# All five engines of a fused HGRN2 and PReLU kernel in one new written order, DMA issues included

## The chip, the core and the metric

The kernel runs on one core of a Trainium2 chip. Its five engines work side by side, each through its own instructions in order: TensorE (PE, with its weight loads shown apart as PEld), VectorE (DVE), ScalarE (ACT), GpSimd (POOL) and SyncE (SP). SP issues only DMA transfers; POOL issues most loads of inputs and two transfers a step that add in flight; ACT issues a few transfers. The metric is device microseconds (us) from launch to end, lower is better.

## The reference

Inputs are `q`, `k`, `v`, `f_logit` of shape (4, 8, 768, 48), `w_in` (384 x 2048), `w_out` (2048 x 384) and `alpha` (2048). In fp32:

```python
f = 1.0 / (1.0 + np.exp(-f_logit))
for t in range(S):                                   # 768 positions
    state = f[:, :, t, :, None] * state + np.einsum('bhd,bhe->bhde', k[:, :, t], v[:, :, t])
    y[:, :, t] = np.einsum('bhd,bhde->bhe', q[:, :, t], state)
x = y.transpose(0, 2, 1, 3).reshape(3072, 384)
h = x @ w_in
g = np.maximum(h, 0.0) + alpha * np.minimum(h, 0.0)
return g @ w_out
```

## The kernel before

**Steps.** The 768 positions are cut into six chunks `c` of 128, the four batch entries into two pairs `bp` (U = 2). That makes twelve steps, numbered 0 to 11, chunk by chunk and within it pair 0 and pair 1; a step covers 256 tokens with all eight heads. The state of a pair lives in 48 partitions of the tile `vs0` or `vs1`, beside the 64 positions of `v` of a half chunk, so that one product gives both the part from earlier positions and the part from these.

**The attention of a step**, in the letters of the order: `e` loads f, q, k, v (POOL; SP in step 0). `f F g G h i k l q p` are decays, scans and scaled copies of q and k (ACT and DVE). `r0 r1` (line 582), `u0 u1` (L591, in the first two steps also L681) and `o` (L566) are PE products of q and k for pairs of positions at growing distance; their results go from PSUM through masked copies on DVE (`R`: L599; `U`: L451 or L702) or copies on ACT (`O`: L573; `H`: L688) into `ad` and `A` (`A`: L606). `K` turns the scaled keys by way of DRAM (four transfers `turned`, one `ksn`, all on SP); in steps 0 and 1 it is a copy on ACT of PE transposes (`k`: L713, `K`: L719). `d` (L539) multiplies them with `v`, `D` and `M` (L550, L554) move the state on. `y0`, `y1` (L614) are the final products for the pair's first and second batch entry, 32 matmuls each, both into one PSUM tile `py`; `Y0`, `Y1` (L494, in steps 0 and 1 L729) are the ACT copies of them into the tile `y`. `X` brings `y` into the layout `xT` in which PE needs it: by three PE products and three ACT copies in step 0 (L738, L747), by ten small transfers over SP, ACT and POOL in steps 1 and 11 (L626), else by two transfers to `tokens` in DRAM and one back (L503, L505, all SP).

**The dense part of a step**, letters after an `N`. `a0` to `a7` (L831) are eight products of `xT` with blocks of `w_in`, 12 matmuls of 256 columns in two instructions each, into a PSUM bank `ph`. `r` (L854) is the ACT part of the PReLU, `c` (L859) the two DVE instructions that finish it into `gate`. From step 3 on blocks 3 to 6 are done in three cheaper rounded passes: `x y z` (L817, L820) split `xT` on ACT, `Y Z` (L823) are POOL transfers that add to `xl` and `xs`, `a` does the first two passes, `q` (L844) scales the bank, `b` is the third pass. The second layer is 64 matmuls `p` (L866, banks `po`) in step 0. From step 1 on it is seven block products `p0` to `p6` (L886, banks `pa` to `pf`) with DVE sums `m u v w` ahead (L880) and `d e f h i j l L` behind (L896); `k g` (ACT), `s0 s1` (SP) finish and store. Weights come in eight pieces each: `a`, `b` hold the transfer (SP) and two ACT conversions (L281, L282), `w`, `v` the DVE sum (L291); `W Y Z` prepare sums and rounded parts of the weights once.

**What sets the order.** `ORDER_WORDS` is a list of such words, a step's number and a letter. Each word calls a function that issues all its instructions at once. The words stand in one list, and PE, DVE and ACT get their instructions in that order:

```python
with tc.manual_schedule(engines={mybir.EngineType.PE, mybir.EngineType.DVE, mybir.EngineType.Activation}):
```

POOL and SP are left to the framework's scheduler. PSUM is eight banks: two rotating pairs (`raw`, `qu`, `off`, `pd`, `py`) and four rotating banks (`ph`, `po`, `pa` to `pf`, `xt`). Waits come from the framework: an instruction waits for the last writer or reader of the tile that it touches.

Words `I` and `J` of step 0 are matmuls on a constant tile (L935), without use for the result. Work of step n+1's attention is mixed into step n's dense part throughout, so that PE always finds a product.

Of the kernel before, what the change touches and what calls it, by code (L numbers as in the profile page):

```python
# [53 lines left out]
4p 3Na1 3Nz 3Na0 4i 3Nr0 2NL 2Ni 4k 4l 3NY 3Na2 4q 3Nr1 3Na7 4K 3Na3 5e 2Ns1 3Nr2 3Nc0 3NZ 3Na4 3Nc2 4t 3Nc1 3Nr7
3Nm0 4u0 3Nc7 4R0 4U0 3Nq3 3Na6 4r1 4A0 4R1 3Na5 4u1 4U1 3Nq4 3Nq5 3Nq6 4o 4O 3Nb3 3Nr3 3Nc3 3Nb4 3Nm1 2Ns0 3Nb6
3Nb5 4d 3Nr4 3Nr5 4D 3Np0 4A1 3Nr6 3Nc6 3Nc5 4y0 3Nc4 4y1 3Np2 5f 4M 4Y0 4Y1 3Np1 3Nk 5F 4X 5g 3Np3 3Nu0 3Nu1 3Nv0
5G 3Nv1 3Nw0 3Ng 3Np4 4Nx 4Ny 3Nw1 3Nd 3Ne 5h 3Nj 3Np5 3Np6 3Nh 3Nf 3Nl 5p 3Ni 5r0 4Nz 4Na0 5i 4Nr0 4Na1 3NL 5k 4NY
4Na5 5l 4Nq5 4Na2 5q 4Nr1 5K 4Na3 4Nc0 4Nr2 5u0 5t 4Nc1 4Nm0 4Nc2 5R0 5U0 4Na7 4Nr7 4NZ 4Na4 6e 3Ns1 5r1 4Nc7 4Nq4
4Nq3 5A0 5u1 5R1 5U1 4Na6 4Nb5 4Nb3 5o 4Nq6 4Nr3 5d 5O 4Nc3 4Nb4 5A1 4Nm1 5D 4Nr4 4Nr5 4Nb6 4Np0 4Nr6 5y0 4Nc4 4Nc5
6f 4Nc6 5y1 5Y0 6F 4Np2 5Y1 5X 6g 4Nk 4Np1 4Np3 4Nu0 4Nu1 4Nv0 4Nv1 4Ng 6G 5Nx 5M 4Nw0 4Np4 5Ny 4Nw1 4Nd 3Ns0 4Ne 6h  # L60
4Nj 4Nh 4Np5 4Nf 4Nl 6p 4Ni 5Nz 5Na0 4Np6 6i 5NY 6k 5Nr0 5Na1 4NL 6l 5Na2 6q 5Na7 5Nr1 6t 5Nc1 6u0 5Nr2 5Nc0 6r0
5Nm0 5Nc2 6R0 5Nr7 5NZ 7e 4Ns1 5Na4 6K 5Na3 6U0 5Nc7 5Na5 6r1 5Nq3 6A0 6u1 6R1 6U1 5Nq4 5Nb3 5Nq5 5Na6 5Nb4 6o 5Nr3
5Nq6 5Nc3 6O 6A1 6d 5Nm1 5Nb6 6D 5Nb5 5Nr4 5Nr5 5Np0 5Nr6 5Nc4 5Nc6 7f 6y0 5Nc5 5Nk 7F 6y1 6Y0 5Np2 6Y1 5Np1 6X 7g
5Np3 5Nu0 5Ng 7G 5Nu1 5Nv0 5Nv1 5Nw1 5Np4 6Nx 5Nw0 5Nd 6M 5Ne 6Ny 7h 5Nj 5Nh 5Np5 5Nf 5Np6 4Ns0 7p 5Ni 6Nz 6Na0 5Nl
7i 7l 6NY 6Nr0 6Na1 5NL 7k 7q 6Na2 6Nr1 7t 6Nc1 6Nr2 6Nc0 6Na7 6Nm0 7K 6Na3 6Nq3 7r0 6Nc2 7u0 7R0 6Nr7 6NZ 6Na4 8e
5Ns1 7U0 6Nc7 6Nq4 6Na5 7u1 7r1 6Nq5 7A0 7R1 7U1 6Na6 6Nq6 6Nb3 6Nr3 6Nc3 6Nb4 6Nm1 6Nb6 6Nb5 7A1 7o 6Nr4 6Nr5 6Nc4
6Nr6 7d 8f 6Np0 7O 6Nc5 7D 6Nk 6Np1 7y0 8F 7y1 6Nc6 7Y0 6Np2 7Y1 7X 8g 7Nx 7M 6Np3 6Nu0 6Nu1 6Np4 6Nv0 6Nd 6Nv1 6Nw0
6Ng 8G 7Ny 6Ne 6Nj 6Nw1 8h 6Nh 6Np5 6Nf 7NY 6Np6 5Ns0 6Nl 8p 6Ni 8i 7Nz 7Na0 7Nr0 7Na1 7Nr1 6NL 8k 8l 7Na2 8t 8r0
7Nr2 7Nc0 8q 7Nc1 8R0 9e 6Ns1 8K 7Na3 7Nm0 7Na7 8u0 7Nc2 7Nr7 7NZ 7Na4 8U0 7Na5 7Nq3 7Nq4 7Nc7 8r1 8u1 7Nq5 8A0 7Na6
8R1 7Nb4 7Nb3 8U1 7Nq6 7Nr3 7Nc3 7Nm1 7Nb6 7Nb5 8o 8A1 8d 7Nr4 7Nr5 7Nc4 7Nr6 8D 8O 9f 7Np0 7Nc5 7Nk 7Np1 7Nc6 8y0  # L70
9F 8y1 8Y0 8Y1 7Np2 8X 9g 7Nd 8M 7Np3 7Nu0 7Nu1 8Nx 7Ne 7Np4 7Nv1 7Ng 9G 8Ny 7Nv0 7Nw0 7Nw1 7Np5 7Nh 9h 7Nf 7Nj 9r0
7Np6 6Ns0 7Nl 9p 7Ni 9R0 8Nz 8Na0 8Na7 9i 8Nr0 8Na1 7NL 9k 9l 8Na2 9q 8Nr1 8NY 8Nr2 9t 8Nc0 8Nc2 8Nc1 8Nr7 8NZ 8Na4
10e 7Ns1 8Nm0 9u0 9U0 9K 8Na3 8Na5 8Nq4 9A0 8Nq3 9u1 9r1 8Na6 8Nc7 9R1 9U1 8Nq5 8Nq6 8Nb3 8Nb4 8Nr3 8Nc3 8Nm1 8Nb6
8Nb5 8Nr5 9o 8Nr4 8Nc5 9A1 8Nr6 9O 9d 8Np0 8Nc4 9D 8Nk 8Np1 8Nc6 10f 9y0 9y1 8Np2 10F 9Y0 9Y1 9X 10g 9M 8Np3 8Nu0
8Nu1 10r0 8Np4 8Nd 9Nx 8Nv0 8Nv1 8Nw0 8Ng 10G 8Np5 8Ne 8Nw1 9Nz 10h 9Ny 8Nh 8Nj 8Nf 10p 8Np6 7Ns0 8Nl 8Ni 9NY 9Na0
9Nr0 8NL 10i 9Na1 9Na2 10k 10l 9Na7 10q 10t 9Nr1 9Nr2 9Nc0 9Nc2 9Nc1 9Nr7 9NZ 9Na4 11e 8Ns1 10R0 10K 9Na3 9Nm0 9Nc7
10u0 9Na5 10U0 9Nq3 9Nq4 9Nb4 9Nq5 9Na6 10A0 9Nq6 9Nb3 10r1 9Nr3 10u1 9Nc3 10R1 9Nm1 9Nb6 9Nr4 9Nb5 9Nr5 9Np0 10U1
# [23 lines left out]
def kernel(  # L101
# [845 lines left out]
    with tc.manual_schedule(engines={mybir.EngineType.PE, mybir.EngineType.DVE, mybir.EngineType.Activation}):  # L947
# [10 lines left out]
        for key in ORDER:  # L958
            run[key]()
# [55 lines left out]
```

## Time and profile before

| | |
|---|---|
| median of 3 runs | 594.9 us (594.26 to 598.04) |
| span of the profiled execution | 592.1 us |
| time around the span (median less span) | 2.8 us |
| PE busy in the span | 580.1 us (98%) |
| DVE, ACT, POOL busy | 505.7, 300.4, 68.4 us |
| mean granted PE clock | 0.988 |
| first `ph` matmul starts | 42.70 us |

The page gives no time of its own for the profiled execution beside its span; 594.9 - 592.1 = 2.8 us is taken as what lies around it. A row of the group list reads: line, engine, operation, output from inputs, shape, count, then busy time, mean ns of one, idle time ahead of it and what ended that.

### The profile page before, as it was taken

The page shows a single profiled execution, that of the slowest core. Times are in us where ns is not written, and L with a number is a line of the kernel's source. Part 1 is how long each engine was busy: PE and PEld are TensorE (multiplying, and loading weights), DVE is VectorE, ACT ScalarE, POOL GpSimd, SP SyncE. Part 2 cuts the span into 40 slices and gives each one's busy share as a digit, 9 for nine tenths or more (in the row PEclk, how much of TensorE's full clock was granted, in tenths as well). Part 3 has the DMA queues.
Part 4 walks back from the last instruction along what each step waited for, and adds up shares of the span by engine and source line. Part 5 has one row for each costly group of instructions (what it writes and reads, how often), then busy time and mean ns, then how long its engine had stood idle before and what let it go on. Part 6 is the DMA issues. An engine that isn't in the chain of part 4 may idle for free.

```text
span 592.1 us, 18853 instructions
## 1 busy us (share of the span) xinstructions
PE 580.1 (98%) x8200; PEld 527.9 (89%) x8200; DVE 505.7 (85%) x1027; ACT 300.4 (51%) x561; POOL 68.4 (12%) x114
## 2 busy tenths in 40 slices
PE   8799999999999999999999999999999999999997
PEld 6678767899899999999999999899899999899997
DVE  7889799899999989899989889989989979966243
ACT  5697973461472473483382374374275355443230
POOL 9110010000101101111111101101100100100100
PEclk9689999999999999999999999999999999999999
DMA  9959212612523823724624614722732731611300
GB/s 299 356 160 348 98 22 63 172 30 86 123 86 91 191 78 89 172 65 105 169 60 106 153 68 106 164 74 85 148 110 81 152 110 54 112 44 30 80 2 27
DMA packets 69443, 67.57 MB, mean 114 GB/s; under 512 B 44688, under 2 KB 58640, under 8 KB 69360
## 3 DMA queue, kind: packets, MB, share of 16 engines
q1 hardware_dynamic: 59744, 37.16, 22.1%
q0 software_dynamic: 8880, 28.84, 19.2%
q8 instruction: 64, 1.05, 0.7%
q10 hardware_dynamic: 736, 0.37, 0.2%
q14 instruction: 19, 0.16, 0.1%
HBM read 44.99 MB, written 13.50 MB: 99 GB/s over the span
## 4 chain that ended last, share of the span: by engine, by line
PE 80%; issue 10%; DMA 4%; ACT 3%; DVE 3%; POOL 1%; POOLq 0%; ACTq 0%; DVEq 0%
PE ph L831 36%; PE pa L886 9%; PE pd L886 5%; PE pf L886 5%; PE pe L886 5%; PE pb L886 5%; PE pc L886 4%; PE py L614 3%; PE qu L591 3%; PE raw L582 3%; DMA w_out_raw<-in_w_out 2%; PE pd L539 1%; PE off L566 1%; DVE ad L451 1%; DMA f<-in_fT 1%
## 5 line engine op out<-in xcount | busy, mean ns | idle before, releaser
L831 PE MATMUL ph<-xT,w_in_sb 128*128 128x256 f32 x612 | 137.1, 380 | 0.2 <-DMA xT<-y 0.2
L831 PEld LDWEIGHTS ph<-xT,w_in_sb 128*128 128x128 f32 x612 | 115.1, 190 | 16.9 <-issue 0.9
L854 ACT ACTIVATE gate<-ph 128x512 f32<-128x512 f32 x96 | 54.6, 594 | 134.4 <-PE ph L831 127.5
L859 DVE SCALAR_TENSOR_TENSOR gate<-gate,om,ph 128x256 f32<-128x256 f32 x192 | 81.0, 476 | 25.6 <-ACT gate L854 25.1
L886 PE MATMUL pa<-w_out_sb,gate 128*128 128x192 f32 x352 | 61.7, 329 | 0.0
L880 DVE TENSOR_TENSOR gate<-gate 128x512 f32<-128x512 f32 x88 | 57.6, 690 | 3.2 <-PE pb L886 2.4
L886 PEld LDWEIGHTS pa<-w_out_sb,gate 128*128 128x128 f32 x352 | 57.1, 190 | 0.5
L599 DVE COPY_PREDICATED ad<-mraw,raw 128x256 f32<-128x256 int32 (+1 forms) x96 | 42.7, 445 | 8.9 <-PE raw L582 6.2
L451 DVE COPY_PREDICATED ad<-mquad,qu 128x224 f32<-128x224 int32 (+6 forms) x140 | 42.2, 302 | 6.8 <-PE qu L591 1.7
L606 ACT COPY A<-ad 32x256 f32<-32x256 f32 x96 | 38.7, 403 | 11.8 <-DVE ad L451 10.4
L440 DVE TENSOR_TENSOR scores<-scores,fs 128x768 f32<-128x768 f32 (+5 forms) x60 | 37.4, 623 | 1.6
L844 ACT ACTIVATE ph<-ph 128x512 f32<-128x512 f32 x36 | 20.2, 574 | 34.0 <-PE ph L831 25.2
L831 PE MATMUL ph<-xh,hi 128*128 128x256 f32 x216 | 34.4, 295 | 0.0
L831 PE MATMUL ph<-xl,lo 128*128 128x256 f32 x216 | 32.0, 283 | 0.3 <-issue 0.3
L886 PE MATMUL pb<-t,gate 128*128 128x192 f32 x176 | 31.2, 331 | 0.0
L831 PEld LDWEIGHTS ph<-xh,hi 128*128 128x128 f32 x216 | 28.7, 190 | 2.8 <-issue 1.6
L424 ACT COPY A<-q 48x512 f32<-48x512 f32 x44 | 27.2, 617 | 7.8 <-DVE q L398 7.2
L886 PE MATMUL pd<-t,gate 128*128 128x192 f32 x176 | 30.7, 328 | 0.3 <-DVE gate L880 0.3
L886 PE MATMUL pc<-t,gate 128*128 128x192 f32 x176 | 30.6, 327 | 0.0
L886 PE MATMUL pf<-w_out_sb,gate 128*128 128x192 f32 x176 | 30.5, 327 | 0.0
L323 POOL DMA_DIRECT2D vs<-in_v x22 | 13.2, 605 | 149.4 <-PE py L614 149.1
L886 PE MATMUL pe<-w_out_sb,gate 128*128 128x192 f32 x176 | 30.4, 326 | 0.0
(153 smaller groups left out, 1044.0 us busy)
## 6 DMA issues: line engine op xcount, KB each, us to landing
w_out_raw<-in_w_out SPq DMA_DIRECT2D x8, 767.8 KB, 9.6
w_in_raw<-in_w_in SPq DMA_DIRECT2D x8, 767.2 KB, 9.5
q<-in_qT POOLq DMA_DIRECT2D x11, 512.0 KB, 5.1
f<-in_fT POOLq DMA_DIRECT2D x11, 512.0 KB, 5.2
k<-in_kT POOLq DMA_DIRECT2D x11, 512.0 KB, 4.2
turned<-f SPq DMA_DIRECT2D x40, 128.0 KB, 4.4
ksn<-turned SPq DMA_DIRECT2D x10, 512.0 KB, 3.5
out<-o SPq DMA_DIRECT2D x24, 192.0 KB, 1.9
```

The source lines that it names most:

```text
L424: nc.scalar.copy(A[halves(cc)[1], :, par * HP:(par + 1) * HP, CH * cc:CH * (cc + 1)], x["q3"][rows(par)].rearrange("p (u h c) s t -> p u h ...
L440: nc.vector.tensor_tensor(by_four(us[:, :, UO[m]:UO[m] + 4 * n]), by_four(us[:, :, skip:skip + 4 * n]), spread(fq[:, :, 1:1 + n], n), ALU. ...
L451: nc.vector.copy_predicated(ad[:, u, :, :, 4 * m:DB], mquad[:, lo:lo + n].bitcast(I32).unsqueeze(1).unsqueeze(1).broadcast_to((128, 2, HP, ...
L582: nc.tensor.matmul(raw[DB * j:DB * (j + 1), par, hp * C:hp * C + QW], lhsT=x["k"][r_, g * DB:(g + 1) * DB], rhs=qd[r_, g], start=True, sto ...
L599: nc.vector.copy_predicated(adu[:, :, :, d:4], mraw[:, d, :, d:4].bitcast(I32).unsqueeze(1).broadcast_to((128, H, NB, n)), rv[:, :, QO[d]: ...
L606: nc.scalar.copy(A[s_, u, :, s_], ad[s_, u].rearrange("p r h t -> p (r h) t"))
L831: nc.tensor.matmul(banks[f][:, j * T:(j + 1) * T], lhsT=of[:, kt, 128 * j:128 * (j + 1)], rhs=by[:, kt], start=first_ and kt + j == 0, sto ...
L844: nc.scalar.activation(banks[f], banks[f], AF.Copy, scale=1.0 - 1.0 / EPS)
L854: nc.scalar.activation(to, of, AF.Relu, scale=-1.0)
L859: nc.vector.scalar_tensor_tensor(to[:, j], to[:, j], om[:, m:m + 1], of[:, j], ALU.mult, ALU.add)
L880: nc.vector.tensor_tensor(block(to)[:, p], block(x_)[:, p], block(y_)[:, p], op)
L886: nc.tensor.matmul(banks[to][:, 0:DH], lhsT=block(of)[:, f], rhs=of_w_out(by)[:, f], start=start and f == 0, stop=f == NH - 1, skip_group_ ...
```

## The change

The kernel computes the same with the same instructions: 4434 on PE, 1027 on DVE and 561 on ACT before and after, and the same transfers. Four things differ.

First, `ORDER_WORDS` is replaced by a list about twice as long, in which a word may stand several times: the functions become generators, and each time that a word stands in the list one more instruction (or one more small group) of it is issued. Instructions of two words on one engine can so alternate. Second, the word `e` is split into `ef`, `eq`, `ek`, `ev`. Third, tiles are made when first needed (`Later`), so that a word may come ahead of the one that used to make its tile. Fourth, POOL and SP follow the list too.

```diff
+class Later(dict):
+    def __missing__(self, key):
+        self[key] = self.make[key]()
+        return self[key]
...
+class Word:
+    def __init__(self, part):
+        self.part, self.left = part, None
+    def __call__(self):
+        if self.left is None:
+            got = self.part()
+            self.left = got if hasattr(got, "gi_frame") else iter(())
+        next(self.left, None)
...
     def lags(raw, u):
...
         for d in range(4):
+            if d:
+                yield
             n = 4 - d
             nc.vector.copy_predicated(
...
         def third():
             gated(bp, c, x)
+            yield
             keyed(bp, c, x)
...
-    with tc.manual_schedule(engines={mybir.EngineType.PE, mybir.EngineType.DVE, mybir.EngineType.Activation}):
+    with tc.manual_schedule(engines={mybir.EngineType.PE, mybir.EngineType.DVE, mybir.EngineType.Activation,
+                                     mybir.EngineType.Pool, mybir.EngineType.SP}):
...
-            x = {}
+            x = Later()
...
+        run = {key: Word(part) for key, part in run.items()}
         for key in ORDER:
             run[key]()
```

Some of the new list, the places that the prediction speaks of (the old list has `1u1 1s 2f 1U0 0Nc7 b6 1U1 1H0 1A0 2F 1t 0Np0 v4 0Np1 0Np2 v5 1d`, `1X` ahead of `0No0 2h 1M 0No1`, `2y0 2y1 1Np3 2Y0 2Y1`, `3y0 3y1 4F 3Y0 2Np2 1Ns0 3Y1` and `6y0 5Nc5 5Nk 7F 6y1 6Y0`):

```diff
+... 0Na6 b2 1p 1q 1p 0Nr7 1t b6 1u1 1u0 1U1 1U1 1K0 1ev 1d 0Np0 b2 v2 ...
+... 1y0 v6 1A1 v4 2h 1A1 1A1 2G 2G 2p b5 1y1 1Y1 b7 2h 0Np4 v5 2g 1Y0 2p 1X 1X 0Np5 0Np6 V
+0Nc7 2q 2q 2q 1X 1X 1X b7 v7 1X 1X 1X 1s 1M 2i 1M 1M 3ef 2i 2q 0Np7 W0 W2 2u0 3ek 2r0 2i 2R0 1X ...
+... 2O 2y0 2Y0 2y1 2Y1 3F 3g ...
+... 3y0 3Y0 3y1 3Y1 4F 4F ...
+... 6y0 6A1 5Nr6 5Nc6 7F 7F 6Y0 6y1 5Nc6 ...
```

## The prediction

> **What bounds the kernel now.** I read the page's head first, then the table of windows, then PE's waits, then the rows of the groups that the new order moves.
>
> ```profile
> span 592.1 us, 18853 instructions
> PE   580.1 (98%) x8200; PEld 527.9 (89%) x8200; DVE 505.7 (85%) x1027; ACT 300.4 (51%) x561; POOL 68.4 (12%) x114
> ```
>
> PE is busy for 580.1 of 592.1 us. PE's busy time is modelled, but the next view has the same answer.
>
> ```profile
> 13.00:16.00 3.00, 1.65 (x8) 1.11 (x6) 3.00 (x7) 3.00 (x5) 3.00 (x4) 1.00 1.04 398
> 16.00:19.00 3.00, 0.99 (x66) 0.91 (x67) 2.94 (x7) 2.40 (x6) 1.39 (x3) 0.99 1.03 394
> 19.00:22.00 3.00, 3.00 (x76) 2.47 (x76) 2.92 (x7) 0.58 (x2) 0.00 (x0) 0.50 1.04 387
> 32.00:34.00 2.00, 1.32 (x4) 0.80 (x4) 2.00 (x5) 1.89 (x6) 0.00 (x0) 0.85 0.54 209
> 40.00:60.00 20.00, 20.00 (x253) 17.52 (x243) 19.38 (x36) 16.67 (x26) 1.45 (x2) 1.00 0.91 323
> ```
>
> The columns are the window and its length, the busy time of PE, PEld, DVE, ACT and POOL, the granted PE clock, the DMA share and GB/s. All of PE's holes lie ahead of 43 us. From there PE is full, but DVE is nearly full beside it (19.38 of 20): PE bounds, and DVE is so close behind that an order can make PE wait for it.
>
> ```profile
> PE off_0a L566 <- DVE kh L402: 2.8, 1, 2.8
> PE idle L935 <- POOL ones L201: 1.6, 1, 1.6
> PE py L614 <- ACT ad L688: 0.8, 1, 0.8
> PE off L566 <- issue: 0.7, 1, 0.7
> PE pk_0a L713 <- DVE ks L406: 0.5, 1, 0.5
> PE py L614 <- ACT y L729: 0.5, 1, 0.5
> PE pd L886 <- DVE gate L880: 0.3, 1, 0.3
> PE ph L831 <- DMA xT<-y: 0.2, 1, 0.2
> ```
>
> Each line is what PE waited for, in total, times, longest. All waits make 8 us, of them under 2 after the first `ph` at 42.7 us. PE's work is the same before and after. So an order can win only from the 42.7 us ahead of `ph`, the 3.5 us behind PE's last matmul (588.6 us), and what PE pays for changing between kinds of product; it can lose anywhere.
>
> **The change part by part.** I placed each instruction of the new order by its waits and summed the rows of before between a product that releases a chain and the product that needs it.
>
> *Start: -0.3.* The chain to the first `ph` ends in three ACT copies to `xT`. In the new order two ACT words more stand ahead of the third copy (weight conversion L282, 0.8, and L281/L365 work), but four ACT and two DVE instructions fewer ahead of the first. By rows the first `ph` starts as if at 42.4. Bounds -2 and +1: the DVE instructions moved by up to three places (0.7 each).
>
> *Changing between kinds of product: -1.5.* A group of 16 second-layer matmuls takes 2.80 us when another kind stands ahead and 2.60 when its like does:
>
> ```profile
> 119.22 2.80 PE pa L886 x16
> ```
>
> The new list has 23 runs of such groups for 30, but 34 runs of fp32 `ph` for 24 and 45 of the rounded ones for 27. Rows of 0.2 lost or won at each kind of change give -2.7; none of it coming gives 0. I take -1.5.
>
> *DVE: 9.3 us less work, worth nothing by itself.* A DVE instruction that reads what the one right ahead wrote starts 0.12 later (L599: 0.48 for 0.36 from start to start). Such neighbours fall from 310 to 234: 76 x 0.12 = 9.3 of DVE's 505.7 us. PE's fullness hides it; without that cover it would count wherever DVE decides.
>
> *`inc` behind `qu0` in step 1: +2.4.* The rows:
>
> ```profile
> L702 DVE COPY_PREDICATED ad<-mhalf,qu 128x224 f32<-128x224 int32 x4 | 1.6, 409 | 2.0 <-PE qu L681 1.9
> L702 DVE COPY_PREDICATED ad<-mhalf,qu 128x128 f32<-128x128 int32 x4 | 1.2, 294 | 0.2
> L291 DVE TENSOR_TENSOR w_out_sb<-w_out_sb,w_out_lead 128x768 int16<-128x768 int16 x8 | 8.1, 1055 | 0.0
> L688 ACT COPY ad<-qu 16x128 f32<-16x128 f32 x16 | 4.1, 255 | 1.1 <-DVE ad L702 0.8
> L494 ACT COPY y<-py 128x512 f32<-128x512 f32 x20 | 10.7, 587 | 19.3 <-PE py L614 19.3
> ```
>
> `1d` now needs the PSUM pair of the product `1u1` two words earlier. That pair is free after three masked DVE copies (0.41, 0.29 and 0.23, two of them dependent), with a weight sum (1.06) and L418 (0.17) between, some 2.3, and then four L688 copies and an L606 copy on ACT, 1.4: 3.7 us. PE has only `1u0` in between, 0.8 for L591 and 1.1 for L681: it waits 1.9. In the old list twelve `po` instructions (3.9 us) covered this. The first `po` behind it waits for L859 behind five further DVE instructions, another 0.3, and the K copy ahead costs 0.2. Behind PE's stall DVE and ACT work on, so nothing else comes late by it. Bounds: 1 and 4.
>
> *The tenth `xT` transfer of step 1: +1.1.* In before all ACT issues of `X` stood ahead of `o0`, `o1`. Now the last word `1X` is behind both, and ACT takes its instructions in order: two copies that wait for the end of `po` (0.49 each), 0.1 to 0.2 ahead, then the issue. From the start of an ACT issue to landing the trace has 3.5 to 4.1 (88.70 to 92.28 for the last). So it lands 4.6 to 5.2 after `po` ends if the issue lies on the way whole, 3.9 at least. PE has a `qu` (0.8), a `raw` (0.85) and four instructions of `ph` (0.9), with a change 2.8. I take 1.1; bounds 0.5 and 2.4. Queued behind it on ACT: the L854 of this `ph`, which would wait anyway.
>
> *`Y0` ahead of `y1` in steps 2, 3 and 6: +2.2.* Both entries' products are in one tile, so `y1` now waits for the ACT copy of `y0`. In before this order stands only in step 0, and the wait of 0.5 on L729 above shows it, with useless matmuls covering another part: from the end of `y0` at 35.26 to the start of `y1` at 36.42 are 1.16 us, twice the copy's 0.587. No PE word stands between in these three steps. Bounds 0.6 and 1.16 each; 0.7 for steps 2 and 3, nearer to the copy since ACT is idle there, and 0.8 for step 6, where ACT has other words ahead.
>
> *DVE chains near their limit: +0.7.* Nine chains of the new list (a masked copy to `off`, `qu` or `ph4`) need 0.05 to 0.25 more by rows than PE's work beside them lasts. The same sums on the old list, where the trace shows no stall, reach -0.04, so the method is good to some 0.3. Sum 0.5 to 1; 0 and 3 as bounds.
>
> *`xl` of step 8: +0.5.* From the end of `y1` to the first product that reads `xl` PE has 15.4 us of work, 21.7 or more in before. The chain is Y copies with L365 words between (2.1), two `tokens` (0.65 each, 3.3 to land), `xT` 3.2, L817 0.84, L820 0.75, POOL's issue 0.9 and 4.0 to land: 16.3. Stalls ahead may have spent part of it, so half: 0 to 1. Other steps have 17.1 or more; the chain of `ksn` needs 10.4 and has at least 11.0. POOL's loads stand in a similar order as before, with the slack of a step.
>
> *End: -0.2.* The last PE word is a half of `pa` with an ACT copy and one store behind it, for a DVE sum and two stores.
>
> Sum: -0.3 - 1.5 + 2.4 + 1.1 + 2.2 + 0.7 + 0.5 - 0.2 = +4.9. The span becomes 592.1 + 4.9 = 597.0. The runs' median lies 2.8 above the span, so 599.8 us.
>
> **Rivals.** *About even, 594 us.* The stalls don't add up: one gives DVE and ACT time, so that later chains come in time. Then the first one (2.4) remains, with the gains of 2.0 against it, and the y waits shrink to 0.6: between 592 and 596.5. For it: the slack of most steps. Against: the y waits lie between PE and ACT alone and cannot be prepaid.
>
> *Faster, 589 us: the clock stays up at the start.* In the windows above PE is idle for most of 14.65 to 18.77 us and the clock drops to 0.50 from 19 to 33 us; PE then runs without a hole, 13 us long. Its products on the way to `xT` (two `qu` with L681 of 3.0 each, `pd` 1.5) would be half as long at full clock: 3.7 us less. In the new list `off` needs DVE's instruction 17, not 20, which is some 2.4 earlier, so that the hole of 2.8 nearly closes. [...] With -3.7 and half the stalls, 594.9 - 3.7 - 2 + 3.5, and lower if the stalls are covered: 587 to 593. For it: the hole is named first among the waits. Against: DVE is busy for 2.92 of 3 us in these windows and sets the pace, and `qu` needs DVE's 26th instruction in both lists, so the hole moves behind `pk`. By the Trainium skill, TensorE: Matmul & The Clock Gate, section What's actually happening, the gate falls to half after one idle window of about 3.4 us, opens after one busy one, and the windows run freely; the drop at 19 us here agrees, and by that rule a shorter hole could keep the gate open or not, by where the window falls.
>
> *Much slower, 612 us: queues in written order.* POOL and SP now issue by the list, where a transfer that waits holds up all behind it. POOL's L323 waited 149 us for `py` in before without harm. If a load or an `xl` comes behind such a wait by 1.5 us in each of ten steps, that is +15. It decides where the slack of 15.4 to 20 us for `xl` is spent. Against: I found only step 8 short.
>
> **How the numbers follow.** Forecast (597 to 604) 0.50, even (592 to 597) 0.24, faster (586 to 592) 0.12, much slower (604 to 620) 0.14. A measurement here tells about 1% (5.9 us) from no change. Faster by over 1%, under 589: most of the third rival, 0.10. Slower by over 1%, over 600.9: 0.14 and half of the forecast's, with 0.23, 0.37. Within: 0.53. The range leaves out 0.08 of the fast and 0.1 of the slow side: 588.5 to 610; the forecast's own range is 597 to 604.
>
> **What would show it.** Right: PE waits for ACT `y` (about 0.7) in steps 2, 3 and 6, for ACT or DVE `ad` ahead of step 1's `inc`, for DMA `xT<-y`; PE's busy time within 3 us of 580.1; DVE's busy sum some 9 lower; first `ph` at 42 to 43 us. Wrong: a clock of 1.00 from 19 to 33 us with `ph` near 39; PE waits below 8 us in all; or long waits of PE for `xl`, `f` or `ksn`.

## The result and the profile after

The new order is slower: median 618.75 us of four runs (616.65 to 619.88) beside 594.64 us for the kernel before, ratio 1.0385 (95% interval 1.0349 to 1.0421). The prediction was 599.8, its range ended at 610. The profiled execution took 619.88 us with a span of 618.0, so 1.9 lie around the span, not the 2.8 that the prediction took.

The head of the page after, the same lines as before:

```profile
span 618.0 us, 18831 instructions
PE 589.6 (95%) x8200; PEld 535.5 (87%) x8200; DVE 498.2 (81%) x1027; ACT 304.1 (49%) x561; POOL 67.7 (11%) x114
```

The span grew by 25.9, PE's busy time by only 9.5. So most of the growth is PE standing idle, and the rest is PE being busy for longer with the same products. The table of windows shows which is which (window and length; busy time of PE, PEld, DVE, ACT, POOL; granted PE clock; DMA share; GB/s):

```profile
40.00:60.00 20.00, 20.00 (x279) 17.31 (x278) 18.27 (x35) 17.62 (x32) 2.66 (x4) 1.00 0.89 298
66.00:76.00 10.00, 8.58 (x161) 6.06 (x159) 7.28 (x18) 8.66 (x17) 0.00 (x0) 0.66 0.01 2
174.00:186.00 12.00, 9.38 (x89) 8.54 (x88) 6.43 (x13) 5.51 (x13) 0.00 (x0) 0.72 0.14 34
```

From 40 to 60 us PE is as full as before. Behind that come stretches in which PE has holes and, in them or just behind, a granted clock below 1: these two, and 314.7 to 318.1 and 403.5 to 406.9 us. In the kernel before the clock never fell again after 34 us while PE had work. In the window from 174 us DVE (6.43 of 12) and ACT (5.51) are less full than PE (9.38); in the one from 66 us ACT (8.66 of 10) is about as full as PE (8.58). No engine is saturated, each waits for another. PE's waits, the main ones behind the first `ph` (total, times, longest):

```profile
...
PE py L716 <- ACT y L586: 2.6, 3, 1.2
PE off L662 <- issue: 2.4, 1, 2.4
PE py L716 <- ACT A L671: 2.2, 3, 1.5
PE inc L632 <- DMA ksn<-turned: 1.8, 1, 1.8
...
PE raw L680 <- issue: 1.6, 1, 1.6
...
PE ph L943 <- issue: 1.3, 1, 1.3
PE inc L632 <- DMA vs<-in_v: 1.3, 1, 1.3
PE pa L1001 <- ACT o L1032: 1.0, 1, 1.0
...
PE qu L689 <- issue: 0.8, 1, 0.8
PE inc L632 <- ACT ad L801: 0.6, 1, 0.6
...
```

All of PE's holes behind the first `ph` make 18 us, where the kernel before had 1.6. No single one is large. They fall into five families: the beginning of a block of PE's instructions ("issue", 6.1 behind the first `ph`), DMA transfers and stores late by the order of POOL and SP (`ksn`, `vs`, `o`: 4.0), the first `y`'s copy (2.6), copies to `A` late on ACT (2.4), and small ones (2.8).

For every kernel run I took four numbers from the PE rows and the granted clock of its profiled execution: the start of the first `ph`; the sum of PE's holes from there to its last product; PE's busy time in that stretch; and the time lost to the clock in it (one less the clock, times 2 us, over windows of 2 us). These four belong to one execution, whose span stands beside them; the median and the ratio are of all its runs, and each ratio is to the runs of the kernel before that were taken beside them (their medians are 594.5 to 595.5). The runs of one kernel spread by 1.7 to 6.9 us, so a difference of 3 us between two medians of the new list is hardly more than their spread.

| kernel | median us | ratio to before (95%) | span | first ph | holes | PE busy | lost to clock |
|---|---|---|---|---|---|---|---|
| before | 594.64 | | 592.1 | 42.70 | 1.6 | 544.3 | 0 |
| after | 618.75 | 1.0385 (1.0349-1.0421) | 618.0 | 41.74 | 18.1 | 554.8 | 10.2 |
| pool_sp_free | 611.31 | 1.0293 (1.0242-1.0344) | 610.4 | 45.43 | 13.6 | 548.0 | 1.7 |
| old_list | 642.93 | 1.0808 (1.0783-1.0834) | 643.2 | 42.94 | 38.4 | 558.3 | 18.8 |
| y_swap | 615.71 | 1.0332 (1.0300-1.0364) | 617.1 | 42.83 | 20.0 | 550.9 | 5.1 |
| fetch_shift | 615.65 | 1.0347 (1.0318-1.0377) | 616.0 | 45.24 | 17.4 | 549.9 | 3.4 |
| early_new | 605.94 | 1.0171 (1.0125-1.0217) | 605.3 | 46.68 | 7.6 | 547.6 | 1.7 |
| late_new | 605.23 | 1.0153 (1.0111-1.0195) | 603.5 | 43.54 | 8.7 | 547.9 | 3.4 |
| y_in_before | 603.25 | 1.0122 (1.0075-1.0170) | 603.1 | 43.68 | 6.3 | 549.6 | 5.1 |
| fill | 623.82 | 1.0477 (1.0429-1.0524) | 618.9 | 43.78 | 16.1 | 555.6 | 3.4 |
| mended | 616.17 | 1.0352 (1.0322-1.0382) | 613.6 | 42.20 | 14.8 | 553.2 | 6.8 |
| y_clean | 599.38 | 1.0059 (1.0037-1.0081) | 597.6 | 42.77 | 4.8 | 546.6 | 1.7 |
| start_new | 597.94 | 1.0054 (1.0030-1.0079) | 594.5 | 41.80 | 4.5 | 544.8 | 0 |
| before_shift | 600.03 | 1.0083 (1.0051-1.0116) | 597.2 | 45.00 | 4.1 | 544.6 | 0 |
| mended2 | 614.91 | 1.0296 (1.0247-1.0346) | 610.2 | 42.73 | 14.8 | 549.3 | 3.4 |
| late_free | 615.38 | 1.0316 (1.0266-1.0367) | 612.5 | 42.12 | 17.3 | 549.7 | 3.4 |
| mended_free | 613.57 | 1.0278 (1.0225-1.0330) | 613.8 | 43.49 | 16.6 | 550.2 | 3.4 |
| y_filled | 600.28 | 1.0082 (1.0050-1.0113) | 598.8 | 43.95 | 1.9 | 549.5 | 0 |
| y_in_again | 603.24 | 1.0124 (1.0079-1.0170) | 601.4 | 43.55 | 6.8 | 547.6 | 3.4 |

The second row makes the sum: start 41.74 - 42.70 = -1.0, holes 18.1 - 1.6 = +16.5, PE busy 554.8 - 544.3 = +10.5, and the time behind PE's last product -0.1: the 25.9. The busy time less what the clock lost is 544.5 after and 544.3 before. So PE's busy growth is the clock, nearly: a part of that loss falls into holes, where it costs nothing (much of it in `old_list`, whose difference is 539.5). (`fill` and `y_filled` hold useless products, which explains theirs.)

### The profile page after: what moved, and what is told of

The parts are those of the page before. It is cut to its first block, busy times and chain, and to the rows that moved or that the text cites. A ratio compares the mean times of both kernels' runs of the same rounds, so it can differ in the third digit from the quotient of the medians.

```text
span 618.0 us, 18831 instructions
## 1 busy us (share of the span) xinstructions
PE 589.6 (95%) x8200; PEld 535.5 (87%) x8200; DVE 498.2 (81%) x1027; ACT 304.1 (49%) x561; POOL 67.7 (11%) x114
## 4 chain that ended last, share of the span: by engine, by line
PE 68%; DVE 13%; DMA 7%; ACT 6%; issue 4%; SPq 1%; POOL 0%; DVEq 0%; POOLq 0%; ACTq 0%
PE ph L943 31%; PE pa L1001 6%; PE po L981 4%; DMA q<-in_qT 3%; PE py L716 3%; PE pb L1001 3%; PE pe L1001 3%; PE pc L1001 3%; PE pf L1001 3%; PE pd L1001 3%; PE qu L689 3%; PE raw L680 2%; DVE gate L995 2%; ACT A L708 1%; PE inc L632 1%
## 5 line engine op out<-in xcount | busy, mean ns | idle before, releaser
L943 PE MATMUL ph<-xT,w_in_sb 128*128 128x256 f32 x612 | 140.8, 384 | 0.1
L943 PEld LDWEIGHTS ph<-xT,w_in_sb 128*128 128x128 f32 x612 | 115.1, 192 | 16.6 <-issue 0.5
L974 DVE SCALAR_TENSOR_TENSOR gate<-gate,om,ph 128x256 f32<-128x256 f32 x192 | 85.1, 475 | 44.0 <-ACT gate L967 43.6
L995 DVE TENSOR_TENSOR gate<-gate 128x512 f32<-128x512 f32 x88 | 59.1, 691 | 17.4 <-PE pc L1001 8.6
L542 DVE COPY_PREDICATED ad<-mquad,qu 128x160 f32<-128x160 int32 (+6 forms) x140 | 41.7, 299 | 6.1 <-PE qu L689 2.5
L699 DVE COPY_PREDICATED ad<-mraw,raw 128x256 f32<-128x256 int32 (+3 forms) x96 | 42.2, 441 | 5.0 <-PE raw L680 3.4
L439 ACT COPY scores<-qd 128x256 f32<-128x256 f32 x48 | 29.6, 681 | 13.5 <-DVE qd L406 13.1
L716 PEld LDWEIGHTS py<-A,vs 128*64 128x64 f32 x768 | 25.0, 143 | 10.6 <-ACT A L671 3.1
L716 PE MATMUL py<-A,vs 128*64 128x64 f32 x768 | 27.3, 230 | 6.8 <-ACT y L586 2.6
L1001 PE MATMUL pb<-t,gate 128*128 128x192 f32 x176 | 32.9, 342 | 0.2 <-DVE gate L974 0.2
L943 PE MATMUL ph<-xs,sum 128*128 128x256 f32 x216 | 31.7, 293 | 1.3 <-issue 1.3
L1001 PEld LDWEIGHTS pb<-t,gate 128*128 128x128 f32 x176 | 30.1, 199 | 1.0 <-DVE gate L974 0.5
```

Source lines behind the costliest of these rows:

```text
L439: nc.scalar.copy(x["q4"][:, :, :, r], qdv[r][:, :, :, 0])
L542: nc.vector.copy_predicated(ad[:, u, :, :, 4 * m:DB], mquad[:, lo:lo + n].bitcast(I32).unsqueeze(1).unsqueeze(1).broadcast_to((128, 2, HP, ...
L699: nc.vector.copy_predicated(adu[:, :, :, d:4], mraw[:, d, :, d:4].bitcast(I32).unsqueeze(1).broadcast_to((128, H, NB, n)), rv[:, :, QO[d]: ...
L716: nc.tensor.matmul(py[64 * par:64 * par + 64, u, o:o + CH], lhsT=vs[bp][:, cc, u, hd * D:hd * D + 64], rhs=A[:, u, par * HP + hp, CH * cc: ...
L943: nc.tensor.matmul(banks[f][:, j * T:(j + 1) * T], lhsT=of[:, kt, 128 * j:128 * (j + 1)], rhs=by[:, kt], start=first_ and kt + j == 0, sto ...
L974: nc.vector.scalar_tensor_tensor(to[:, j], to[:, j], om[:, m:m + 1], of[:, j], ALU.mult, ALU.add)
```

## Experiments

**The queues of POOL and SP.** Two kernels take the two halves of the change apart. The first is the new list with its engines cut back (their names are shortened in these code cuts):

```diff
-    with tc.manual_schedule(engines={PE, DVE, Activation, Pool, SP}):
+    with tc.manual_schedule(engines={PE, DVE, Activation}):
```

> The new list for PE, DVE and ACT, but POOL and SP ordered by the framework's scheduler as in before. Theory A (each hole of PE in the profile after has its own cause): the three waits of PE that come from POOL's and SP's order go (1.75 for ksn in step 4, 1.27 for vs in step 9, 1.01 for the o buffer in step 10, 4.0 together), the rest stays: 612 to 616 us. Theory B (the written order of POOL and SP is what costs): back to 595 to 600 us.

The second is the new code with the old list, each word run to its end at once, `e` written as `ef eq ek ev`:

```diff
-        next(self.left, None)
+        for _ in self.left:
+            pass
```

> The old list, word for word and instruction for instruction on PE, DVE and ACT, in the new code, with POOL and SP following that list too. Theory A: POOL and SP by the list cost no more than 4 us: 594 to 598 us. Theory B: 608 us or more.

The first took 611.31 us, a little better than A's 612 to 616: the waits for `vs` and `o` are gone, and of that for step 4's keys 0.4 is left, now called "issue"; the time is 7.4 us less, in spite of a start that is 3.7 later. In the profiled execution the holes are 4.5 less and the clock lost 8.5 less. So about 17 of the 24 us are left with scheduled queues. The second took 642.93: with PE, DVE and ACT in exactly the old order, the written order of POOL and SP alone makes +48. PE's longest wait of it, then one of DVE's:

```profile
PE pd L972 <- DVE gate L966: 19.5, 3, 8.5
```

```profile
DVE o L982 <- DMA out<-o: 35.2, 6, 10.2
```

A store stands on SP behind transfers that wait; DVE, in order, waits to reuse the tile that the store still reads; the `gate` sums behind it are late; PE waits 19.5 us for them, and 10.7 more for late `xs` transfers of POOL. The rival "queues in written order" was thus real, with the old list far more than with the new: the new list places its DMA words much better than a plain listing of the old words does. In the new kernel a small case of it is visible at step 4 (SP rows, start and length):

```profile
209.04 0.58 SPq L568 DMA_DIRECT2D turned<-f  x1
209.67 0.66 SPq L874 DMA_DIRECT2D out<-o  x1
210.77 5.34 SPq L568 DMA_DIRECT2D turned<-f  x3
220.12 0.34 SPq L571 DMA_DIRECT2D ksn<-turned  x1
```

A store stands between the key transfers, and from the first of them to the landing of `ksn` at 224.00 are 15.0 us, where the prediction reckoned 10.4 and the ten steps of the kernel before have 10.0 to 12.4. The store isn't all of it: in `mended` and `mended2` below it stands behind the keys, and the same way takes 14.9 and 14.5, since `ksn` itself then lands 6.4 and 6.0 us behind its issue instead of 3.9. With scheduled queues it is 12.1 (`pool_sp_free`).

**The first `y`'s copy ahead of the second `y`.** First the pairs turned back in the new list, then the same pairs turned in the kernel before.

```diff
-... 2O 2y0 2Y0 2y1 2Y1 ...   -... 3y0 3Y0 3y1 3Y1 ...   -... 7F 6Y0 6y1 ...
+... 2O 2y0 2y1 2Y0 2Y1 ...   +... 3y0 3y1 3Y0 3Y1 ...   +... 7F 6y1 6Y0 ...
```

> The new list with y1 ahead of Y0 in steps 2, 3 and 6, nothing else. Theory A: the three waits of PE for the ACT copy of y (0.69, 0.68, 1.19) go, 2.6 us; if the clock's fall at 178 us hangs on the wait of step 3 too, another 3.4: 612.5 to 616.5 us. Rival (the time freed is waited for at the next late chain): 618 to 619 us.

```diff
-... 2y0 2y1 1Np3 2Y0 ...   -... 4f 2Nd T 3y0 3y1 4F 3Y0 ...   -... 7f 6y0 5Nc5 5Nk 7F 6y1 6Y0 ...
+... 2y0 2Y0 2y1 1Np3 ...   +... 4f 2Nd T 3y0 3Y0 3y1 4F ...   +... 7f 6y0 5Nc5 5Nk 7F 6Y0 6y1 ...
```

> The kernel before with one edit, the copy of the first y put ahead of the second y's product in steps 2, 3 and 6, which in the new list cost PE holes of 0.69, 0.68 and 1.19. Theory A (such a wait between PE and ACT alone is paid in full): three holes of 0.6 to 1.2, 2.2 to 2.6 more, so 596.9 to 597.3, and up to 3.4 more for each hole that closes the clock. Rival B (absorbed by waits that shrink): 594.7 within 0.5.

`y_swap` took 615.71, 3.0 less, in A's range, but its runs (612.94 to 618.96) overlap the new kernel's. Its three holes are gone, yet all its holes sum to 20.0, more than the new kernel's 18.1. Its profiled execution was the slowest of its four, with a span 0.9 shorter than the new kernel's: 1.9 more in holes, 1.1 more at the start, 3.9 less of PE's busy time, where the clock lost 5.1 for 10.2. `y_in_before` took 603.25, 8.4 more than the kernel before beside it. B falls; A's 596.9 to 597.3 needs two falls of the clock on top, which came (5.1 lost), but two of the holes are far above its 0.6 to 1.2. The ACT rows at step 3 say why:

```profile
174.56 0.85 ACT L795 ACTIVATE sum<-xh 128x768 fp32r<-128x768 f32 x1
...
176.77 0.84 ACT L795 ACTIVATE sum<-sum 128x768 fp32r<-128x768 f32 x1
177.51 0.57 ACT L493 COPY y<-py 128x512 f32<-128x512 f32 x1
```

`y0` had ended at 175.26, but ACT had four weight sums of word `T` to do ahead of the copy, from 174.56 on: PE's hole is 2.88, not 0.7. In step 6 it is 1.86, by the three `f` instructions ahead; in step 2, where ACT was idle, 0.69. (These rows are of the kernel's second run, `y_in_again`; the first had 2.87, 1.85 and 0.69.) The next kernel puts these ACT words behind the copy:

```diff
-... 4f 2Nd T 3y0 3Y0 3y1 4F ... 3Y1 3M   -... 7f 6y0 5Nc5 5Nk 7F 6Y0 6y1 ...
+... 4f 2Nd 3y0 3Y0 3y1 4F ... 3Y1 T 3M   +... 6y0 5Nc5 5Nk 6Y0 7f 7F 6y1 ...
```

> The kernel before with the first y's copy ahead of the second y's product in steps 2, 3 and 6, as in the run that took 603.25, but with the ACT words that stood ahead of that copy (four weight sums of T in step 3, the three f instructions in step 6) put behind it. Theory A (the hole is the ACT queue ahead of the copy and not the copy): holes of 0.7, 0.7 and 0.7 for 0.69, 2.87 and 1.85, no clock closed behind them, 596 to 597.5. Rival B (the wait itself upsets what follows): 600 and above.

```profile
PE py L613 <- ACT y L493: 2.1, 3, 0.7
...
PE off L565 <- issue: 1.4, 1, 1.4
```

Three holes of 0.69, 0.68 and 0.68, as A said. The time is 599.38, between the ranges of A and B, since two holes with no releaser ("issue") grew, from 0.69 and 0.35 to 1.42 and 0.70, and the first closed the clock. The price of this order is thus 0.7 where ACT is free, and whatever ACT holds ahead where it isn't.

**Holes without a releaser: instruction blocks.** In the new kernel `off` of step 6 stops after 56 of its 64 products:

```profile
310.60 0.68 PE L662 MATMUL off<-q,kh 48*32 48x32 f32 x56
313.66 0.27 PE L662 MATMUL off<-q,kh 48*32 48x32 f32 x8 [2.38 <-issue]
```

The page's part on DMA queues has a queue of instructions:

```profile
q8 instruction: 64, 1.05, 0.7%
```

Its 64 packets carry 16,384 bytes each, and PE has 64 times 256 instructions (8200 loads and 8200 products): a packet is a block of 256, or 128 load and product pairs. One packet starts at 311.06, and PE goes on 2.6 us later; the other such holes of the new kernel lie in the same way 2.2 to 2.6 behind a packet (65.53 to 67.83, 361.36 to 363.96, 400.46 to 402.65). If the blocks cause them, a shift of the stream must move them. `fetch_shift` is the new kernel with 56 pairs more at the start; `fill` (its other part below) with 128 pairs more ahead of them; `before_shift` is the kernel before with 56 pairs more (its expectation says fewer, but its trace has 8256 products for 8200).

```diff
-IDLE, BEFORE, BEHIND = 14, 6, 8
+IDLE, BEFORE, BEHIND = 10, 6, 8
         for _ in range(IDLE):
             idled(idle, 0)
+        for _ in range(32):
+            nc.tensor.matmul(idle[0:32, 0:32], lhsT=ones[0:48, 0:32], rhs=ones[0:48, 0:32], start=True, stop=True)
```

> The new list with 32 useless 32x32 matmuls more and 4 useless words of 256 columns fewer at the very start, which moves all later PE instructions by 56 pairs of load and matmul against the blocks of 256 instructions (16 KB) in which they are fetched. Theory A (PE's holes of 2.38, 1.30 and 1.58 us at 311, 363 and 401 us, put down to issue, are fetches of instructions that come too late): these holes go or move to other products, and with them the two falls of the clock behind them (3.4 each): 606 to 614 us, unless other boundaries fall badly. Rival (a wait that the profile doesn't show): the same products have the same holes, 618 us.

> The kernel before with 56 load and product pairs fewer ahead of everything behind the start (IDLE 10 for 14 and 32 tiny products added), so that the blocks of 256 instructions begin at other products. Theory A (a hole without a named releaser lies where a block begins among small products): the holes of 0.69 at 208 and 0.35 at 343 go and others come elsewhere or not, 593 to 597. Rival B (no link to the blocks): the same two holes stay at the same products.

In the new kernel the holes stood behind PE's 4284th, 4918th and 5427th products. Shifted by 56 they were gone, and others came (1.68 at 351, 2.84 at 358, a 3.66 in the start), so that the time hardly changed: 615.65, above A's range. Shifted by 128, one whole block, they were back behind products 4412, 5046 and 5555: the same three, 128 further. In the kernel before the two holes went as well and others came (1.23 at 213, 1.07 at 399, 0.85 at 162, more in the start): 600.03, A's mechanism, three above its range, of which the first `ph`, 2.3 later, is the larger part. So the blocks make these holes, but most of the 64 blocks make none. Three of the new kernel's four stand in runs of small products (64 in some 0.9 us); why just these blocks come too late isn't shown.

**Does a hole close the clock?** `fill` puts useless products into two holes of the new kernel, and 53 tiny ones (as in the diff above, with IDLE 10) at the start, which makes 128 pairs more in all.

```diff
+        for _ in range(8):   # step 4, ahead of d's products, into the same bank
+            nc.tensor.matmul(pd[:, 0, 0:256], lhsT=ones[:, 0:128], rhs=ones[:, 0:256], start=True, stop=True)
+        for _ in range(7):   # step 3, ahead of y0, into the bank of y
+            nc.tensor.matmul(x["py"][:, 0, 0:256], lhsT=ones[:, 0:128], rhs=ones[:, 0:256], start=True, stop=True)
```

> The new kernel with useless matmuls where PE has nothing: seven of 256 columns ahead of step 3's y0 and eight ahead of step 4's d products (the holes of 1.9 and 1.75), 53 tiny ones at the start and IDLE 10 for 14, so that the instruction blocks behind begin at the same products as in the new kernel. Theory A (holes of about 2 us close the clock): the fall at 178 to 185 us is gone and the kernel 3.4 faster than the new one, 614 to 616, while the holes filled bring nothing by themselves. Rival B (the clock falls for another reason, the filling only costs): 618 to 620.

It took 623.82, outside both ranges: ill made. The seven products waited themselves for the copies to `A` (a hole of 1.55 stayed), and the useless products took 0.45 to 0.47 each, 6.9 us in all. The fall at 178 us was gone, but the holes of 1.54 and 0.40 ahead of it had become the one of 1.55. A clean test fills the holes of `y_in_before`, between `y0` and `y1`, in columns that nobody reads:

```diff
+            for _ in range({3: 13, 6: 8}.get(n_, 0) * u):
+                nc.tensor.matmul(x["pd"][:, 0, 384:512], lhsT=ones[:, 0:128], rhs=ones[:, 0:128], start=True, stop=True)
```

> The kernel before with the y order turned (603.25; holes of 0.69, 2.87 and 1.85 at y1, clock falls behind the last two, 5.6 lost less 0.9 at the end), with useless products of 128 columns between y0 and y1, 13 in step 3 and 8 in step 6, in columns that nobody reads: y1 still waits as long for the first y's copy, but PE is not idle. Theory A (holes close the clock): no fall at 176 to 186 and 316 to 322 us, some 4.7 less, 598 to 600. Rival B (the clock falls there for another reason): the two falls stay, 602.5 to 604.

> The kernel with the y order turned once more, for comparison on the same chip: 602.5 to 604.5, with one or two falls of the clock behind the holes of 2.87 and 1.85.

The windows of the unfilled kernel, then of the filled one:

```profile
176.00:182.00 6.00, 3.87 (x38) 3.75 (x39) 4.28 (x8) 3.93 (x8) 1.21 (x2) 0.61 0.09 15
182.00:186.00 4.00, 4.00 (x20) 4.00 (x19) 1.07 (x3) 1.23 (x3) 0.00 (x0) 0.72 0.60 175
```

```profile
176.00:182.00 6.00, 6.00 (x70) 5.81 (x69) 4.68 (x8) 4.60 (x9) 1.21 (x2) 1.00 0.11 24
182.00:186.00 4.00, 4.00 (x85) 3.66 (x84) 3.41 (x6) 1.21 (x3) 0.00 (x0) 1.00 0.56 162
```

`y1` starts no sooner (178.56 beside 178.13), yet the clock stays at 1.00 and the kernel is 3.0 us faster, 600.28 beside 603.24, both in A's ranges. An idle PE closes the clock: the fall behind the hole of 2.88 loses 3.4 us, more than the hole itself. The hole of 1.86 closed it in one profiled execution of the unfilled kernel and not in the other; that of 2.88 did in both.

**Halves.** With POOL and SP scheduled, the new list up to some 199 us and the old order behind, and the reverse:

```diff
-ORDER = flat()
+ORDER = new words up to 3Na0, then the rest in the old order          # early_new
+ORDER = old words up to 3Na1, then the rest in the new order          # late_new
```

(The added lines are in words here; the code has the list itself.)

> The new list for PE, DVE and ACT up to the last words of step 2 (some 199 us), from there the old order; POOL and SP by the scheduler. To be held against the new list with POOL and SP by the scheduler, 611.3 us, and the kernel before, 594.7. Theory A (the loss is a sum of PE holes and clock falls, each made at its own place): the new part has 5.0 us of holes ahead of 199 us, one fall of the clock of about 3 and a first ph 2.7 to 3.3 later than in the kernel before, so 603 to 607. Rival B (the loss is made behind 199 us, or holes ahead of it are won back later): 595 to 598.

> The old order for PE, DVE and ACT up to the first a products of step 2's dense part (some 188 us), from there the new list; POOL and SP by the scheduler. Theory A (a sum of holes, each made at its own place): 611.3 less 5.0 of holes, 3 of clock and 2.7 of the later start: 600 to 604, and its excess over 594.7 and that of the other half add up to the whole excess of 16.6 within 3. Rival B (the loss is all ahead of 188 us): 595 to 598; rival C (all behind): 608 and above.

605.94 and 605.23: 11.1 and 10.4 above the kernel before, together 21.5 where the whole has 16.6. Neither half is to blame alone, B and C fall; the late half is 1 above A's 600 to 604. The excess is 5 beyond the whole, not within 3 as expected: the two first `ph` are later by 4.0 and 0.8, together 2.1 more than that of the whole.

**The start.** `start_new` keeps the new list, with all five engines written, up to the first `ph`; `late_free` is the new list throughout, POOL and SP written only up to there.

```diff
-        for key in ORDER:
+        for key in ORDER[:first_a]:
             run[key]()
+    with tc.manual_schedule(engines={PE, DVE, Activation}):
+        for key in ORDER[first_a:]:
+            run[key]()
```

> The new list with all five engines in written order up to the first ph, the old order from there, POOL and SP by the scheduler from there. Theory A (the new start is worth what the first ph says, 42.70 to 41.74): 593.5 to 594.2. Rival B (the later ph only takes the time back, or the start of the old order behind it lacks words): 594.7 to 597.

> The new kernel with POOL and SP in written order up to the first ph only, and by the scheduler from there. The fully scheduled one took 611.3 with its first ph at 45.43, 3.7 later than the new kernel's 41.74. Theory A (what the written queues cost behind the start is 7 to 11 us, and the later start was lost by the scheduler): first ph near 41.8, 606.5 to 609.5. Rival B (the later start is taken back by later waits, so that it never counted): 610.5 to 612.

`start_new` has its first `ph` at 41.80 as expected by A, but took 597.94, above both ranges: the `ph` behind it come sooner than what they need (its longest wait behind the first `ph`; another of 0.9 is for `w_in_sb`):

```profile
PE ph L943 <- DVE gate L974: 1.9, 1, 1.9
```

`late_free` took 615.38, 4.1 more than with the later start, outside both ranges: at 68.60 PE waits 1.8 for `inc <- ACT ad`, and its holes are 17.3 for 13.6. In both the earlier first `ph` came back as holes at least as long (2.8 more for 0.9 in `start_new`, 3.7 more for 3.3 in `late_free`), at once in `start_new`, late in `late_free`: that one is still 3.5 us ahead of `pool_sp_free` at 149 us and loses 2.1 of it in step 3, where ACT waits 4.3 for a load of `f` and PE has holes of 0.61, 0.59 and 0.40, and the rest behind 309 us. `start_new` also bounds what the new code itself can cost, with its late tiles and split loads: it has that code, nearly the old list and scheduled queues behind the start, and is 2.7 above the kernel before beside it.

**Mending hole by hole.** `mended` edits the new list; its product `p2` of step 2 stands ahead of the words that finish blocks 6 and 7 of `gate`, so that it reads their old values, all instructions being there: it has the new kernel's work but computes something else, and its time serves for this comparison alone.

```diff
-... 2y0 2Y0 2y1 2Y1 ... 1Np3 ...   -... 3y0 3Y0 3y1 3Y1 ... 2Np2 ...   -... 1d 0Np0 ...   -... 4d 3Nb4 ...
+... 1Np3 2y0 2y1 2Y0 2Y1 ...       +... 2Np2 3y0 3y1 3Y0 3Y1 ...       +... 0Np0 1d ...   +... 3Nb4 4d ...
-... 10ef ... 9ev ...   -... 11X (x8) ... 9Ns1 11X ...   -... 2Ns1 ... 4K ...   -... 6Y0 6y1 ...
+... 9ev 10ef ...       +... 9Ns1 11X (x10) ...          +... 4K 2Ns1 ...       +... 6y1 6Y0 ...
```

> The new kernel with its single PE holes mended one by one in the list: the second y ahead of the first y's copy in steps 2, 3 and 6 (2.56 us of holes), a second-layer block moved ahead of the y of steps 2 and 3 (2.4), step 4's d products and the store on SP behind the keys (1.75), step 9's v load ahead of the f load that waits (1.27), step 9's store ahead of the ten transfers of step 11 (1.01), step 1's d products behind one po (0.59). Theory A (a sum of holes, each made and mended at its own place): 9 of 18.1 us of holes go, and two of the four falls of the clock, 3 to 7: 603 to 607. Rival B (time won at one place comes back as a hole at the next, as when the y order alone was changed): 612 to 617.

616.17, so B. Two of its edits made new holes right behind: the blocks moved ahead of `y` are then missing as cover, and PE waits for the bank that DVE or ACT still reads:

```profile
PE pd L1001 <- DVE o L1011: 2.3, 1, 2.3
...
PE pa L1001 <- ACT o L1032: 1.9, 1, 1.9
```

`mended2` mends the same holes on ACT, POOL and SP instead; `mended_free` is the same list in the form of `late_free`.

```diff
-... 1Nk 2A1 3g 3ev 3F 2O 2y0 2Y0 2y1 ...
+... 2A1 2O 1Nk 3g 3ev 3F 2y0 2y1 2Y0 ...
-... T 3o 3O 3O 3A1 2Nc3 4ev 2Nr6 3d 3D 3D 1Ns0 2Nc3 4F 2Nc6 2Np0 3O 3O 3A1 3A0 3y0 3Y0 3y1 3Y1 ...
+... 3o 3O 3O 3A1 3O 3O 3A1 3A0 2Nc3 4ev 2Nr6 3d 3D 3D 1Ns0 2Nc3 4F 2Nc6 2Np0 3y0 3y1 3Y0 3Y1 T ...
```

and `4d` behind `3Np0`, with `6y1`, `9ev`, `9Ns1` and `2Ns1` as in `mended`.

> The new kernel with its holes mended on ACT, POOL and SP, and PE's products left in place but for two: the copies to A ahead of weight sums, gate and scores work on ACT in steps 2 and 3 (2.4 us of holes), the second y ahead of the first y's copy in steps 2, 3 and 6 (2.56), step 4's d products behind the first po-like block and the store behind the keys on SP (1.75), step 9's v load ahead of the waiting f load (1.27), step 9's store ahead of step 11's ten transfers (1.01). Theory A (holes with causes of their own): 18.1 us of holes become 9 to 11, one to three of the four falls of the clock go, 603 to 609. Rival B (little slack: a hole taken away comes back at the next place): 612 to 617.

> Both together: the mended list on PE, DVE and ACT, POOL and SP written up to the first ph and scheduled from there. Theory A (holes add up): the run with the scheduled queues (606.5 to 609.5) less 2.56 for y, 2.4 for the copies to A and one to two clock falls of 3.4: 598 to 603. Rival B (they come back): 606 or above. Neither theory has it below the kernel before, 594.7, since about 5 us of waits for the beginning of instruction blocks stay.

614.91 and 613.57: both B. In `mended2` the aimed holes are gone or small (step 3's `y` 1.54 to 0.74), and the clock lost 3.4 for 10.2, but waits grew or came elsewhere: 1.76 for 0.59 at `inc` in step 1, 0.90 for `gate`, 3.03 for 2.38 at the block in step 6. In `mended_free` PE's holes are 16.6. No version of the new list, and no small edit of the old one, came below the kernel before.

## Why the prediction was wrong, point by point

**The step that failed** is "I placed each instruction of the new order by its waits and summed the rows of before between a product that releases a chain and the product that needs it", read as finding all the places. Where it named a place it was near: the `y` waits 2.56 for 2.2, 0.69, 0.68 and 1.19; `inc` in step 1 0.59 and an "issue" of 0.84 just ahead for 2.4; DVE's sum 7.5 less for 9.3 (76 x 0.12 is 9.1); waits for DVE's `o`, `ad`, `gate` and `scores` 2.0 for 0.7, of which only 0.6 (`ad`, `scores`) are the masked copies it named; the start -1.0 for -0.3; the end -0.1 for -0.2. The transfer of `xT` in step 1 and `xl` of step 8 cost nothing (1.6 reckoned). It saw about 4 of the 26. Of its signs, the `y` waits and the one for `ad` came; that for `xT<-y` didn't, PE's busy time grew by 9.5 and not under 3, the first `ph` came ahead of 42, and a wait for `ksn` (1.8) was among its signs of being wrong. What it left out:

- **The copies to `A` on ACT** (2.4, of them 1.94 in step 3). I compared chains with PE's work beside them, but ACT is in order too. ACT's rows ahead of step 3's `y`, where PE waited from 175.46 to 177.00:

```profile
173.92 0.84 ACT L908 ACTIVATE sum<-xh 128x768 fp32r<-128x768 f32 x1
...
175.70 0.60 ACT L967 ACTIVATE gate<-ph 128x512 f32<-128x512 f32 x1
176.32 0.63 ACT L671 COPY A<-off 32x256 f32<-32x256 f32 x2
```

  A weight sum and a `gate` (1.44 together) stand among the copies that `y` needs. But ACT's own order is only a part of it: just ahead, up to 171.60, ACT had stood idle for 1.86 us for a load of `q` that POOL issues. In `mended2`, with these two behind the copies and the wait for `q` as before (1.93), 1.13 of the 1.94 are left; in `pool_sp_free`, with ACT's order unchanged and no wait for `q`, nothing is left. `y_clean` and `y_in_before` show what ACT's queue alone can do, 0.7 against 2.88.

- **POOL and SP** (4.0 of holes; 7.4 of time by `pool_sp_free`). The sentences "POOL's loads stand in a similar order as before, with the slack of a step" and "the chain of `ksn` needs 10.4" are wrong: 15.0 for `ksn`, which needed up to 12.4 even in the kernel before, a load of `v` behind one of `f` that waits for a transfer, and step 3's late `q`. The rival at 612 had a right mechanism with too small a chance; its place, `xl`, was not where it cost. That the measured 618.75 lies in its 604 to 620 is in part luck: scheduled queues take back 7.4 of the 24.

- **Blocks of instructions** (6.1 for 1.0 before). The one "issue" of 0.7 among the waits that I quoted was such a hole; I did not ask what it was.

- **The clock** (10.2). I looked at it for the start alone. A PE hole was priced at its length; by the unfilled kernel one of 2.88 costs 3.4 more than that. And the fall at 19 us in the kernel before, which the prediction took to agree with one idle window, came behind 3.4 us in which PE was idle for 2.5 only.

**Changing between kinds of product**, -1.5, did not come; nor does the -2.7 that it was taken from follow from the counts beside it, 7 runs fewer and 28 more. PE's busy time less the clock's loss is 544.5 for 544.3, and 546 in several kernels of the new list.

**The rival "the clock stays up at the start"** is answered by `start_new`: in its profiled execution the clock lost 1.7 us ahead of 40 us, where the kernel before lost 6.8 and the new kernel 5.1, and the first `ph` still came at 41.80 (41.74 in the new kernel). So the clock doesn't set the start; PE's longest wait ahead of it there is 2.97 for ACT's copy to `A`. **"About even"** rested on stalls that give time back. They do come back, but as other holes: `y_swap`, `start_new`, `late_free` and `mended` each took waits away and got others, at the next place or far behind.

**What stays open**: why the new list has so little slack everywhere, while the old order hides all but 1.6 us. The runs show that its holes have many owners and that neither half, nor POOL and SP alone, nor any few words hold them; they do not show one cause.

## What to carry to other kernels

Before an order on several in-order engines is called even, list for each product of the bounding engine what stands ahead of its releaser on that releaser's own engine, DMA queues included; the length of the releaser alone is only the lower bound (0.7 against 2.9 here). Price a hole of some 2 us or more in a full TensorE at its length and, as the worse case, 3.4 us more for the clock (2.88 cost that; one of 3.19 in `y_swap` cost nothing more), and don't count a start that comes sooner before you have seen that the next chain comes sooner too. An order in which PE already runs without holes has little to win and can lose in small parts at dozens of places; a forecast of such a change should lean to the slow side even where each place that was found is small.

## What the runs showed of the hardware

The clock falls in portions. The time lost to it behind the start was 0, 1.7, 3.4, 5.1, 6.8, 10.2 or 18.8 us, all multiples of about 1.7: a fall to 0.50 lasts about 3.4 us, or a multiple, and within a trace all changes of the clock lie on one grid of 3.41 us. The Trainium skill, TensorE: Matmul & The Clock Gate, section What's actually happening, has a window of about 3.4 us that runs freely, and these portions agree with it. The same page of the Trainium skill, section Why this matters for your kernels, advises against PE gaps of more than about 3 us. Here the length of a gap alone doesn't decide: 2.88 closed the clock in both profiled executions of that kernel, 1.86 in one of them, and in the new kernel it fell at 68.95 behind a hole of 0.84 among small products; yet a hole of 3.19 in `y_swap` (360.80 to 363.99) closed nothing.

The grid tells more than the gap. The 3.19 lay across two portions of it, with 1.25 and 1.94 us of idle PE; the same hole of 1.90 in step 6 closed the clock in `late_free`, where it lay in one portion, and not in `pool_sp_free`, where it was split 0.67 and 1.23. Behind 45 us, in all 19 profiles, all 14 portions at full clock in which PE was idle for 2 us or more were followed by half clock. Below that it went both ways (1.94 and 1.85 each with and without a fall, 0.84 with one); what decides there is not shown.

PE can stop and go on only 2.2 to 2.6 us behind the start of a packet of 256 of its own instructions, with holes of 0.84 to 2.38 us in the new kernel, and the profile calls such a hole "issue". Moving the stream by 56 pairs moves these holes; moving it by 128 puts them back at the same products. So even useless products at the start change the time of a full kernel: 595.3 to 600.0 for the kernel before, with the first `ph` 2.3 later and 2.5 more of holes.
